# Loading two weight rows ahead of a branch, decoding late weights a step later, and moving sums, differences and splits a step sooner

## The chip, the core and the metric

One core of a Trainium2 chip runs the whole program in one launch. The metric is the device time of that launch in microseconds; a lower time is better. Times before are 1471.26 to 1475.34 us over three runs, median 1472.84.

## What is computed

Three layers follow one another on 4608 tokens of width 512:

```python
kv = einsum("bhsd,bhse->bhde", k, v); o = q @ kv; x = o / rms(o) * g_norm     # 8 batches, 8 heads, 576, 64
e = argmax(x @ w_gate + bias[modality]); x = p[e] * (relu(x @ w1[e]) @ w2[e])   # 8 experts, 512 -> 1024 -> 512
out = (sigmoid(x @ w_gate2) * (x @ w_val2)) @ w_out2                            # 512 -> 1536 -> 512
```

The change concerns the third layer, called the output part here, and the way into it. Its three weight matrices come as float64, that is as two 32-bit words an element.

## The kernel before

All matrix products are float32. Each is made of three products of halves: a value is split into a high part (a copy by ScalarE, ACT) and a low part (value minus high part, by VectorE, DVE), and TensorE (PE) multiplies high by high, high by low and low by high.

**Decoding.** The float64 weights are decoded in units of 128 x 512 (class `Decode`): one ACT instruction for the exponent, five on DVE for the words, and a store of 256 KB to `w_d[cb]` in DRAM. Most units are decoded during the expert layer. The last eight, those of `w_d[2]`, are `Late` units: `decode_late` loads the raw words (512 KB, L1646) and `decode_late2` decodes a unit and stores it (L155, L157), during the first steps of the output part.

**The output part** goes over 5 token blocks of 12 steps each, steps 0 to 59 (`NJ` is 12, `FIRST` is 24, `NU` is 60). Step 0 is computed around a branch (`tc.If`, L1206) that holds expert work that is rarely needed and not run here. Each step has eight spots in the order `SPOTS`; at each spot `prepare(s, spot)` issues what later steps need, then PE's product of that spot follows. A step of the first block (`glu_plain`, L984 to L986) is 24 matmuls for gate and value and 12 for the output, all 128 x 512. From the second block on (`glu_unit`, L1010 to L1012) a step computes its two products by seven smaller ones, in the order 1, 6, 7, 5, 2, 4, 3, of 6 matmuls each; DVE adds the banks of PE into `u2`, `u3` and `gm` (L1014).

**Weights.** `load_rows(s + 2)` (L1290) loads 512 KB of decoded weights for step s + 2 from `w_d` into one of two buffers, `rows[s % 2]`, at spot 0 of step s. `group` splits them for the next step into `wt` on ACT (L972) and DVE (L973) and stores the result for later blocks to `wt_d` (L1316). From step 12 the splits are of sums of the rows (`sum_w`, L1306). `load_raw` (L922) loads 256 KB of `w_out`; its split is stored to `wo_d` (L1347). All these transfers, and the loads of the next block's tokens (`load_y`, L1613), are issued by SyncE on one queue (SPq), in the order of the program. Each of them also waits for the transfer that used its lane (`DMAHW0` to `DMAHW7`) before.

**Y sums.** A block from the third on needs seven combinations of its tokens (`y_step`, L1253 for the low part of a split, L1257 for a sum). The table `YPLAN` says at which step and spot each is issued: keys are (step within the block before, spot), letters name the combination. `YPLAN[1]` serves the third block, made in steps 22 to 24. Buffers for the splits come from `free_y`, filled by `hold_y`.

**The tail.** Blocks from the third on have their output in chunks of 12 matmuls 128 x 256 (`run_chunk`, L1488 to L1490), seven kinds n for six pairs m. `ready_chunk` splits a chunk's input (ACT `gh` L1457, DVE `gl` L1450) up to four spots ahead. `sum_g` (L1469, L1470) makes two sums of a pair; for the last block GpSimd (POOL) makes a difference for each pair (L1461 for m below 3, L1472 for the others). `combine` (L1513) adds finished banks into `u2` and `u7`. After step 59 come 24 chunks: n of 2 and 4 alternating for m 0 to 5, then n = 6, then n = 5. In the same stretch `last_split` (L1548) splits the six differences, and `last_products` (L1562 to L1567) ends the program.

What is issued around the late units, with the words of the kernel:

```python
if spot == 0:
    load_wt(s + 1)
    if s + 2 <= NJ:
        load_raw(s + 2, s + 1)
    load_rows(s + 2)
    decode_late(s)
```

Of the kernel before, what the change touches and what calls it, by code (L numbers as in the profile page):

```python
# [25 lines left out]
NB = 5  # L26
# [58 lines left out]
def attention_moe_glu_kernel(  # L85
# [962 lines left out]
    with ExitStack() as st:  # L1048
# [80 lines left out]
        for g in range(2):  # L1129
            later(8 + 2 * g, lambda g=g: split0(g))  # L1130
            later(13 + g, lambda g=g: split1(g))

        def gv_first(at):
# [77 lines left out]
    with ExitStack() as st:  # L1211
# [31 lines left out]
        free_y = []  # L1243
        yslots = []

# [13 lines left out]
        def y_step(b, what):  # L1259


            sub = ALU.subtract
            if what in SPLIT:
                split_y(b, SPLIT[what], {"a": y11, "b": y21, "c": y22, "g": y22, "h": y21, "i": y11, "k": y12}[what])
            elif what == "d":
                sum_y(y22, y22, y12, sub)
            elif what == "e":
                sum_y(y12, y12, y11, sub)
            elif what == "f":
                sum_y(y11, y22, y11, ALU.add)  # L1270
            elif what == "j":
                sum_y(y21, y21, y11, sub)
# [3 lines left out]
                  (11, 1): "h", (11, 3): "k"},  # L1276
                 {(10, 5): "c", (10, 2): "d", (10, 4): "e", (11, 1): "a", (11, 7): "f", (11, 5): "i", (11, 2): "g", (11, 4): "k",
                  (12, 1): "b", (12, 6): "jh"},
                 {(10, 5): "c", (10, 2): "d", (10, 4): "e", (11, 1): "a", (11, 7): "f", (11, 5): "i", (11, 2): "g",
# [142 lines left out]
        def place_chunks(b):  # L1422

            s0 = NJ * b
            early = [(6, 2, 4), (7, 2, 4), (8, 2, 4), (10, 2, 4), (11, 6, 5), (11, 2, 4)]
            if b == NPLAIN:
                early[0:3] = [(7, 2, 4), (8, 6, 5), (9, 2, 4)]
            for m, (j, *spots) in enumerate(early):
                for spot, n in zip(spots, (1, 7)):
                    chunk_at.setdefault((s0 + j, spot), []).append((b, n, m))  # L1430
                sum_at.setdefault((s0 + max(j + 1, 2 * m + 2), (1, 5)[m % 2]) if m < 3 else (s0 + NJ + 1, (1, 5, 4)[m - 3]), []).append((b, m))
            seq = [(b, n, m) for m in range(6) for n in (2, 4)] + [(b, n, m) for n in (6, 5, 3)[0:3 if b < NB - 1 else 2] for m in range(6)]
            for i, c in enumerate(seq):
                chunk_at.setdefault((s0 + NJ + i // 6, SPOTS[1 + i % 6]), []).append(c)
# [7 lines left out]
        def ready_chunk(q):  # L1442
# [16 lines left out]
            split_c[q] = (hi, lo)  # L1459
            if n == (2 if m < 3 else 0) and b == NB - 1:  # L1460
                nc.gpsimd.tensor_tensor(out=g[a12], in0=g[a12], in1=g[a11], op=ALU.subtract)  # L1461
# [5 lines left out]
        def sum_g(b, m):  # L1467
            g = G[b]
            nc.vector.tensor_tensor(out=g[2 * m, 1], in0=g[2 * m, 1], in1=g[2 * m + 1, 1], op=ALU.add)  # L1469
            nc.vector.tensor_tensor(out=g[2 * m, 0], in0=g[2 * m, 1], in1=g[2 * m, 0], op=ALU.subtract)  # L1470
            if b == NB - 1 and m > 2:
                nc.gpsimd.tensor_tensor(out=g[2 * m + 1, 0], in0=g[2 * m + 1, 0], in1=g[2 * m, 0], op=ALU.subtract)  # L1472

# [33 lines left out]
        def combine(b, n):  # L1507
# [24 lines left out]
            if n == 6:  # L1532
# [4 lines left out]
                later_o.extend([lambda: third(0), lambda: third(1)])  # L1537
                later_o.append(lambda: add(held["u7"], held["u7"], held["u2"]))
            if n == 5 and b == NB - 1:
# [123 lines left out]
        def decode_late(s):  # L1663

            for i in ((0, 1) if s == 0 else (s,) if 1 < s < 8 else ()):
                jobs[i] = Late(units[NEARLY + i], i)

        def decode_late2(s):
            if 1 <= s < 9:
                d = jobs.pop(s - 1)  # L1670
                d.exponent()
                d.words()
                d.finish()
                d.store()

        def prepare(s, spot):
# [3 lines left out]
            if spot == 0:  # L1680
                load_wt(s + 1)
                if s + 2 <= NJ:
                    load_raw(s + 2, s + 1)
                load_rows(s + 2)
                decode_late(s)
# [16 lines left out]
            if b + 1 < NB:  # L1702
                for what, do in TURNS[min(b, 1)].get((j, spot), ()):
                    what(b + 1, do)
                if s == 9 and spot == 0:
                    hold_y(mw[1].tile([128, 2, 2, 2, HC], F32R, tag="w2r1", name="w2r1"))
# [11 lines left out]
            sums_o(s, spot)  # L1718
            if (s, spot) == (FIRST, 0):
                yslots.extend(xp.tile([128, XW], F32, tag="xg", name="yr", bufs=4) for _ in range(2))  # L1720
                free_g.extend(xp.tile([128, XW], F32, tag="xg", name="yr", bufs=4)[:, 0:HC] for _ in range(2))
            if s == NU - 1 and spot in SPOTS[1:7]:
# [8 lines left out]
        load_raw(2, 1)  # L1731
        load_rows(2)
        for i in range(4):
            load_y(1, i)
        for i in range(4):
            number_y(1, i)
        decode_late(0)
        ready_o(1, 0)
# [17 lines left out]
        for s in range(NU, NU + 4):  # L1756
            for spot in SPOTS:
                chunk_step(s, spot)
                if s == NU + 2 and spot in SPOTS[1:7]:
                    last_split(SPOTS.index(spot) - 1)  # L1760
        last_products()
# [26 lines left out]
```

## Time and profile before

| what | value |
|---|---|
| median of three runs | 1472.84 us (1471.26 to 1475.34) |
| profiled execution | 1472.33 us |
| its span, first to last instruction | 1470.5 us |
| mean granted clock of PE | 0.992 |
| busy: PE, DVE, ACT, POOL | 96%, 69%, 46%, 18% |
| DMA | 365.34 MB, mean 248 GB/s |

The time of the profiled execution is 1.8 us above its span. The granted clock is a share of PE's full speed. Idle time in a row of the timeline stands in brackets with what ended it.

### The profile page before, as it was taken

The numbers are of one execution on the slowest core, as the hardware profiler recorded it, in microseconds if no ns is written. First come the engines' busy times: TensorE is split into PE (matmuls) and PEld (weight loads), VectorE is DVE, ScalarE is ACT, GpSimd is POOL, SyncE is SP. The second block draws the span as 40 slices with busy tenths as digits, with TensorE's granted clock in tenths as the row PEclk, the third lists the DMA queues.
The fourth block names the chain that finished last, engine by engine and source line by source line (L and its number), as shares of the span: only waits on it lengthen the run. The fifth ranks groups of instructions, "written<-read, shape, count | busy, mean of one in ns | idle before, by whom it ended". The sixth has DMA issues, their size and how long they took to land.

```text
span 1470.5 us, 24842 instructions
## 1 busy us (share of the span) xinstructions
PE 1417.6 (96%) x9302; PEld 1240.9 (84%) x9302; DVE 1009.5 (69%) x1592; ACT 677.6 (46%) x1080; POOL 269.7 (18%) x356
## 2 busy tenths in 40 slices
PE   6997999999999999989999999999999999999996
PEld 6886789999999998778888887888889888898896
DVE  1567868888888877647866676565876468655574
ACT  3676555556555556746433342332433235222241
POOL 1021122223121213111011101011024200131025
PEclk9999999999999999999999999999999999999999
DMA  9987599998985857689887656886666655565553
GB/s 297 332 302 248 184 318 309 267 327 284 302 287 187 289 164 241 235 273 335 317 337 255 243 194 248 327 285 232 208 215 221 207 203 186 196 215 199 193 162 111
DMA packets 189708, 365.34 MB, mean 248 GB/s; under 512 B 22544, under 2 KB 114448, under 8 KB 182416
## 3 DMA queue, kind: packets, MB, share of 16 engines
q1 hardware_dynamic: 177408, 330.37, 66.8%
q0 software_dynamic: 10816, 32.08, 6.0%
q8 instruction: 75, 1.23, 0.3%
q10 hardware_dynamic: 1360, 1.26, 0.3%
q14 instruction: 49, 0.40, 0.1%
HBM read 301.31 MB, written 74.93 MB: 256 GB/s over the span
## 4 chain that ended last, share of the span: by engine, by line
PE 52%; DMA 2%; DVE 1%; POOL 1%; issue 1%; ACT 0%; SPq 0%; another core or an unknown queue 0%; POOLq 0%; ACTq 0%; DVEq 0%
PE gv L1010 10%; PE gv L1011 10%; PE gv L1012 10%; PE ac L1490 4%; PE ac L1488 3%; PE ac L1489 3%; PE ac L1382 2%; PE ac L1383 2%; PE ac L1384 2%; PE gv L984 1%; PE gv L986 1%; PE gv L985 1%; PE tr L947 1%; DMA wos<-wp_d 1%; DMA rows<-w_d 1%
## 5 line engine op out<-in xcount | busy, mean ns | idle before, releaser
L279 PE MATMUL ph<-xh,w1h 128*128 128x256 f32 x576 | 167.2, 290 | 1.1 <-ACT w1h L235 1.1
L280 PE MATMUL ph<-xh,w1l 128*128 128x256 f32 x576 | 163.5, 284 | 0.9 <-DVE w1l L237 0.9
L281 PE MATMUL ph<-xl,w1h 128*128 128x256 f32 x576 | 163.5, 284 | 0.0
L1014 DVE TENSOR_TENSOR u<-u,gv 128x512 f32<-128x512 f32 x144 | 98.5, 684 | 78.5 <-PE gv L1012 77.8
L1488 PE MATMUL ac<-wos,gh 128*128 128x256 f32 x480 | 135.7, 283 | 2.3 <-ACT gh L1457 1.1
L1490 PE MATMUL ac<-wos,gl 128*128 128x256 f32 x480 | 136.3, 284 | 1.4 <-DVE gl L1450 1.3
L1489 PE MATMUL ac<-wos,gh 128*128 128x256 f32 x480 | 135.9, 283 | 0.0
L1010 PE MATMUL gv<-half,wt 128*128 128x512 f32 x336 | 132.2, 393 | 0.0
L1011 PE MATMUL gv<-half,wt 128*128 128x512 f32 x336 | 131.3, 391 | 0.0
L1012 PE MATMUL gv<-half,wt 128*128 128x512 f32 x336 | 131.0, 390 | 0.0
L279 PEld LDWEIGHTS ph<-xh,w1h 128*128 128x128 f32 x576 | 110.8, 192 | 3.0 <-ACT w1h L235 1.3
L280 PEld LDWEIGHTS ph<-xh,w1l 128*128 128x128 f32 x576 | 110.9, 193 | 2.8 <-DVE w1l L237 1.1
L281 PEld LDWEIGHTS ph<-xl,w1h 128*128 128x128 f32 x576 | 110.6, 192 | 0.0
L335 PE MATMUL py<-w2h,hh 128*128 128x512 f32 x272 | 106.9, 393 | 0.0
L336 PE MATMUL py<-w2l,hh 128*128 128x512 f32 x272 | 106.8, 393 | 0.0
L337 PE MATMUL py<-w2h,hl 128*128 128x512 f32 x272 | 106.0, 390 | 0.0
L1488 PEld LDWEIGHTS ac<-wos,gh 128*128 128x128 f32 x480 | 91.8, 191 | 7.2 <-issue 1.4
L1489 PEld LDWEIGHTS ac<-wos,gh 128*128 128x128 f32 x480 | 91.8, 191 | 3.7
L1490 PEld LDWEIGHTS ac<-wos,gl 128*128 128x128 f32 x480 | 91.8, 191 | 1.9 <-DVE gl L1450 1.8
L349 POOL DMA_INDIRECT y_d<-y,sidx x36 | 40.4, 1122 | 283.2 <-ACT y L345 110.5
L1043 ACT ACTIVATE u<-u 128x512 f32<-128x512 f32 x48 | 30.4, 633 | 134.1 <-DVE u L1014 134.1
L301 ACT ACTIVATE hh<-ph 128x512 fp32r<-128x512 f32 x68 | 40.6, 598 | 105.5 <-PE ph L281 105.5
(408 smaller groups left out, 3736.1 us busy)
## 6 DMA issues: line engine op xcount, KB each, us to landing
wt<-wt_d SPq DMA_DIRECT2D x36, 1536.0 KB
half<-in_moe_w_dram SPq DMA_DIRECT2D x96, 512.0 KB
w1r<-in_moe_w_dram SPq DMA_DIRECT2D x40, 512.0 KB
w2r<-in_moe_w_dram SPq DMA_DIRECT2D x40, 512.0 KB
wos<-wp_d SPq DMA_DIRECT2D x72, 256.0 KB
rows<-w_d SPq DMA_DIRECT2D x24, 512.0 KB
wt<-wt_d SPq DMA_DIRECT2D x48, 256.0 KB
wt_d<-wt SPq DMA_DIRECT2D x12, 1024.0 KB
```

The source lines that it names most:

```text
L279: nc.tensor.matmul(out=o, lhsT=bh[:, c, cs], rhs=hi[:, c, 0:n], start=(c == 0), stop=False)
L280: nc.tensor.matmul(out=o, lhsT=bl[:, c, cs], rhs=hi[:, c, 0:n], start=False, stop=False)
L281: nc.tensor.matmul(out=o, lhsT=bh[:, c, cs], rhs=lo[:, c, 0:n], start=False, stop=(c == KC - 1))
L335: nc.tensor.matmul(out=o, lhsT=hi[:, f, cs], rhs=bh[:, f, :], start=first, stop=False)
L336: nc.tensor.matmul(out=o, lhsT=hi[:, f, cs], rhs=bl[:, f, :], start=False, stop=False)
L337: nc.tensor.matmul(out=o, lhsT=lo[:, f, cs], rhs=bh[:, f, :], start=False, stop=last)
L1010: nc.tensor.matmul(out=o, lhsT=wh, rhs=yh[:, c, :], start=first and c == 0, stop=False, skip_group_check=True)
L1011: nc.tensor.matmul(out=o, lhsT=wh, rhs=yl[:, c, :], start=False, stop=False, skip_group_check=True)
L1012: nc.tensor.matmul(out=o, lhsT=wl, rhs=yh[:, c, :], start=False, stop=last and c == 1, skip_group_check=True)
L1488: nc.tensor.matmul(out=o, lhsT=gh[:, cs], rhs=wh, start=fresh and i % 2 == 0, stop=False, skip_group_check=True)
L1489: nc.tensor.matmul(out=o, lhsT=gh[:, cs], rhs=wl, start=False, stop=False, skip_group_check=True)
L1490: nc.tensor.matmul(out=o, lhsT=gl[:, cs], rhs=wh, start=False, stop=stop, skip_group_check=True)
```

## The change

1. The weight rows of steps 2 and 3 are loaded ahead of the branch (`later(12)` and `later(15)`); the loads of them behind the branch go.
2. The late units are loaded and decoded one step later: the first two raw loads move from ahead of step 1 into step 1, the decoding from steps 1 to 8 into steps 2 to 9, and the buffer that they use becomes free for Y splits at step 10, not 9.
3. For the third block, c, d, e and the sum f (F, now by halves into two buffers `extra_y`) are in step 22, a, I, g, k and b in step 23, and in step 24 only the difference J and its split H.
4. For the last block, the sums of pairs 3 to 5 are issued a step sooner, POOL's six differences all when the chunk n = 2 is made ready, the six last splits over two steps, and the sum of `u7` and `u2` in two halves.

```diff
@@ -1129,6 +1129,7 @@
         for g in range(2):
             later(8 + 2 * g, lambda g=g: split0(g))
             later(13 + g, lambda g=g: split1(g))
+            later(12 + 3 * g, lambda g=g: nc.sync.dma_start(out=rows[g], in_=w_rows(2 + g)))
...
+            elif what == "F":
+                for k in range(2):
+                    sum_y(extra_y[k], y22[:, k], y11[:, k], ALU.add)
+            elif what == "I":
+                hl = free_y.pop(0)
+                for k in range(2):
+                    nc.scalar.activation(out=hl[0][:, k], in_=extra_y[k], func=ACTF.Copy)
+                for k in range(2):
+                    sum_y(hl[1][:, k], extra_y[k], hl[0][:, k], sub)
+                Y[b, 6] = hl
+            elif what == "J":
+                for k in range(2):
+                    sum_y(y11[:, k], y21[:, k], extra_y[k], sub)
+            elif what == "H":
+                split_y(b, 4, y11)
...
-                 {(10, 5): "c", (10, 2): "d", (10, 4): "e", (11, 1): "a", (11, 7): "f", (11, 5): "i", (11, 2): "g", (11, 4): "k",
-                  (12, 1): "b", (12, 6): "jh"},
+                 {(10, 1): "c", (10, 6): "d", (10, 5): "e", (10, 4): "F", (11, 1): "a", (11, 6): "I", (11, 5): "g", (11, 2): "k",
+                  (11, 4): "b", (12, 1): "J", (12, 6): "H"},
...
-                sum_at.setdefault((s0 + max(j + 1, 2 * m + 2), (1, 5)[m % 2]) if m < 3 else (s0 + NJ + 1, (1, 5, 4)[m - 3]), []).append((b, m))
+                late = (s0 + NJ, (6, 5, 4)[m - 3]) if b == NB - 1 else (s0 + NJ + 1, (1, 5, 4)[m - 3])
+                sum_at.setdefault((s0 + max(j + 1, 2 * m + 2), (1, 5)[m % 2]) if m < 3 else late, []).append((b, m))
...
-            if n == (2 if m < 3 else 0) and b == NB - 1:
+            if n == 2 and b == NB - 1:
                 nc.gpsimd.tensor_tensor(out=g[a12], in0=g[a12], in1=g[a11], op=ALU.subtract)
...
-            if b == NB - 1 and m > 2:
-                nc.gpsimd.tensor_tensor(out=g[2 * m + 1, 0], in0=g[2 * m + 1, 0], in1=g[2 * m, 0], op=ALU.subtract)
...
-                later_o.append(lambda: add(held["u7"], held["u7"], held["u2"]))
+                if b < NB - 1:
+                    later_o.append(lambda: add(held["u7"], held["u7"], held["u2"]))
+                else:
+                    h7, h2 = ([held[z][:, 2 * k:2 * k + 2, :] for k in range(2)] for z in ("u7", "u2"))
+                    later_o.extend([lambda: add(h7[0], h7[0], h2[0]), lambda: add(h7[1], h7[1], h2[1])])
...
-            for i in ((0, 1) if s == 0 else (s,) if 1 < s < 8 else ()):
+            for i in ((0, 1) if s == 1 else (s - 1,) if 2 < s < 9 else ()):
                 jobs[i] = Late(units[NEARLY + i], i)
...
-            if 1 <= s < 9:
-                d = jobs.pop(s - 1)
+            if 2 <= s < 10:
+                d = jobs.pop(s - 2)
...
-                load_rows(s + 2)
+                if s > 1:
+                    load_rows(s + 2)
                 decode_late(s)
...
-                if s == 9 and spot == 0:
+                if s == 10 and spot == 0:
                     hold_y(mw[1].tile([128, 2, 2, 2, HC], F32R, tag="w2r1", name="w2r1"))
...
-            if (s, spot) == (FIRST, 0):
+            if (s, spot) == (NJ, 0):
                 yslots.extend(xp.tile([128, XW], F32, tag="xg", name="yr", bufs=4) for _ in range(2))
-                free_g.extend(xp.tile([128, XW], F32, tag="xg", name="yr", bufs=4)[:, 0:HC] for _ in range(2))
+                extra_y.extend(xp.tile([128, XW], F32, tag="xg", name="yr", bufs=4)[:, 0:HC] for _ in range(2))
+            if (s, spot) == (FIRST, 7):
+                free_g.extend(extra_y)
...
-        load_rows(2)
...
-        decode_late(0)
...
-                if s == NU + 2 and spot in SPOTS[1:7]:
-                    last_split(SPOTS.index(spot) - 1)
+                at = (NU + 1, 6), (NU + 1, 5), (NU + 1, 4), (NU + 2, 6), (NU + 2, 7), (NU + 2, 5)
+                if (s, spot) in at:
+                    last_split(at.index((s, spot)))
```

Three places show how this moves instructions. Line numbers of the changed kernel are higher by 1 to 19 for the same statement.

SyncE, before, from the end of step 6 to the start of step 8 of the output part: the store of a late unit (L157), the loads of raw `w_out` and of rows (L922, L1290), a raw late load (L1646) and the two stores of splits.

```order
L157 DMA w_d2_78<-w2r1_8548 128x512 [waits DMAHW5_49,DVE_49]
L922 DMA wo_8969<-w_d1_77 128x512 [waits DMAHW6_49]
L1290 DMA rows0_2674<-w_d2_78 128x1024 [waits DMAHW7_49]
L1646 DMA w2r1_8548<-in_moe2_w_out_dram 128x1024 [waits DMAHW0_49,Activation_49]
L1316 DMA wt_d7_86<-wt1_7729 128x1536 [waits DMAHW1_49,DVE_49]
L1347 DMA wo_d6_97<-wos_9021 128x1024 [waits DMAHW2_49,DVE_49]
L157 DMA w_d2_78<-w2r1_8548 128x512 [waits DMAHW3_49,DVE_49]
L922 DMA wo_9050<-w_d2_78 128x512 [waits DMAHW5_49,DMAHW4_49]
L1290 DMA rows1_2675<-w_d2_78 128x1024
```

The same stretch in the changed kernel, from the end of step 6 to the start of step 8.

```order
L157 DMA w_d2_78<-w2r1_8550 128x512 [waits DMAHW1_49,DVE_49]
L922 DMA wo_9042<-w_d2_78 128x512 [waits DMAHW2_49,DMAHW1_49]
L1306 DMA rows1_2675<-w_d2_78 128x1024
L1665 DMA w2r1_8550<-in_moe2_w_out_dram 128x1024 [waits DMAHW4_49,Activation_49]
L1332 DMA wt_d8_87<-wt0_8528 128x1536 [waits DMAHW5_49,DVE_49]
L1363 DMA wo_d7_98<-wos_9092 128x1024 [waits DMAHW6_49,DVE_49]
L157 DMA w_d2_78<-w2r1_8550 128x512 [waits DMAHW7_49,DVE_49]
L922 DMA wo_9109<-w_d2_78 128x512 [waits DMAHW7_49,DMAHW0_49]
L1306 DMA rows0_2674<-w_d2_78 128x1024
```

Before, the load `wo_9050` waits for lane 5, that of the store in the first row; now each `wo` load that reads `w_d2` waits for the lane of the store in the row ahead of it (lane 1, then lane 7).

DVE, before, in step 22 (`rows`/`wsum` are weights, `yraw` and `half0` the tokens' sums and a split, `u2`, `u3`, `gm` PE's results):

```order
L973 TENSOR_TENSOR wt1_7729<-wsum_10392,wt1_7729 128x2x256
L1014 TENSOR_TENSOR u2_10397<-u2_10397,gv_10410 128x512
L1351 TENSOR_TENSOR gl_10419<-gm5_8533,gh_10418 128x512
L1014 TENSOR_TENSOR u3_10398<-u2_10397,gv_10424 128x512
L1014 TENSOR_TENSOR gm7_8535<-u3_10398,gv_10432 128x512
L1253 TENSOR_TENSOR half0_7669<-yraw_8527,half0_7669 128x1024
L973 TENSOR_TENSOR wt1_7729<-wsum_10392,wt1_7729 128x2x256
L1257 TENSOR_TENSOR yraw_8527<-yraw_8527 128x2x512
L1014 TENSOR_TENSOR gm9_8537<-u2_10397,gv_10424 128x512
L1257 TENSOR_TENSOR yraw_8527<-yraw_8527 128x2x512
L1014 TENSOR_TENSOR u3_10479<-u2_10397,gv_10432 128x512
```

The same stretch in the changed kernel.

```order
L973 TENSOR_TENSOR wt1_7730<-wsum_10388,wt1_7730 128x2x256
L1254 TENSOR_TENSOR half0_7669<-yraw_8529,half0_7669 128x1024
L1014 TENSOR_TENSOR u2_10393<-u2_10393,gv_10408 128x512
L1367 TENSOR_TENSOR gl_10417<-gm5_8535,gh_10416 128x512
L1258 TENSOR_TENSOR yraw_8529<-yraw_8529 128x2x512
L1014 TENSOR_TENSOR u3_10394<-u2_10393,gv_10423 128x512
L1014 TENSOR_TENSOR gm7_8537<-u3_10394,gv_10431 128x512
L1258 TENSOR_TENSOR yraw_8529<-yraw_8529 128x2x512
L973 TENSOR_TENSOR wt1_7730<-wsum_10388,wt1_7730 128x2x256
L1014 TENSOR_TENSOR gm9_8539<-u2_10393,gv_10423 128x512
L1258 TENSOR_TENSOR yr_9380<-yraw_8529 128x512
L1258 TENSOR_TENSOR yr_9381<-yraw_8529 128x512
```

The split into `half0` and the first sum of `yraw` stood behind `u3_10398`; now they stand ahead of its counterpart `u3_10394`, and the two halves of F are new in this step.

DVE, before, in the tail, around the turn from the chunks n = 6 to n = 5 (`w1r1` is a last split, `wos` are `u2` and `u7`):

```order
L1450 TENSOR_TENSOR gl_15592<-wsum_11449,gh_15591 128x512
L1548 TENSOR_TENSOR w1r1_8580<-rows0_11447,w1r1_8580 128x512
L1513 TENSOR_TENSOR wos_11445<-wos_11445,ac0_15500 128x512
L1513 TENSOR_TENSOR wos_11445<-wos_11445,ac1_15501 128x512
L1450 TENSOR_TENSOR gl_15613<-gm10_8538,gh_15612 128x512
L1513 TENSOR_TENSOR ot_15616<-wos_11445,ac2_14735 128x512
L1548 TENSOR_TENSOR w1r1_8580<-gm11_8539,w1r1_8580 128x512
L1513 TENSOR_TENSOR ot_15626<-wos_11445,ac3_14736 128x512
L1513 TENSOR_TENSOR wos_11446<-wos_11446,wos_11445 128x1024
L1450 TENSOR_TENSOR gl_15651<-wsum_11449,gh_15650 128x512
```

The same stretch in the changed kernel.

```order
L1567 TENSOR_TENSOR w1r1_8579<-gm11_8541,w1r1_8579 128x512
L1467 TENSOR_TENSOR gl_15592<-wsum_11445,gh_15591 128x512
L1528 TENSOR_TENSOR wos_11441<-wos_11441,ac0_15502 128x512
L1528 TENSOR_TENSOR wos_11441<-wos_11441,ac1_15503 128x512
L1467 TENSOR_TENSOR gl_15611<-gm10_8540,gh_15610 128x512
L1528 TENSOR_TENSOR ot_15614<-wos_11441,ac2_14731 128x512
L1528 TENSOR_TENSOR ot_15622<-wos_11441,ac3_14732 128x512
L1528 TENSOR_TENSOR wos_11442<-wos_11442,wos_11441 128x512
L1467 TENSOR_TENSOR gl_15647<-wsum_11445,gh_15646 128x512
```

The last split now stands ahead of the adds on `ac0` and `ac1`, and one half of the add of `wos` stands ahead of `gl_15647`, where the whole stood ahead of `gl_15651`.

## Rows read from the trace of the kernel before

**Rows 1.** the page, part 1: busy us of each engine, share of the span
```profile
PE 1417.6 (96%) x9302; PEld 1240.9 (84%) x9302; DVE 1009.5 (69%) x1592; ACT 677.6 (46%) x1080; POOL 269.7 (18%) x356
```

**Rows 2.** timeline, SP's queue, POOL and PE, place A (start, us, engine line op, [idle before <-releaser])
```profile
633.25 1.75 SPq L1613 DMA_DIRECT2D yr<-y_d  x4
...
636.13 0.19 POOL L935 COPY oid<-yr 128x1 int32<-128x1 int32 x1 [7.69 <-DMA yr<-y_d]
...
649.49 1.97 PE L947 MATMUL tr<-ident,yr 128*128 128x128 f32 x8 [3.81 <-ACT yr L942]
```

**Rows 3.** windows: busy us by engine, granted clock, DMA share, GB/s
```profile
640.00:660.00 20.00, 16.19 (x70) 13.30 (x69) 9.91 (x17) 9.81 (x17) 2.21 (x4) 0.91 0.97 338
880.00:900.00 20.00, 16.88 (x63) 13.41 (x62) 12.09 (x17) 7.53 (x12) 4.65 (x7) 0.83 0.59 213
```

**Rows 4.** timeline, DVE and PE, steps 22 and 24
```profile
859.97 0.68 DVE L1014 TENSOR_TENSOR u<-u,gv 128x512 f32<-128x512 f32 x1
861.36 1.22 DVE L1253 TENSOR_TENSOR half<-yraw,half 128x1024 fp32r<-128x1024 f32 x1
...
861.15 0.39 PE L1010 MATMUL gv<-w2r,wt 128*128 128x512 f32 x1
...
886.94 1.22 DVE L1253 TENSOR_TENSOR w2r<-yraw,w2r 128x1024 fp32r<-128x1024 f32 x1 [1.12 <-ACT w2r L1252]
...
888.91 0.77 PE L1010 MATMUL gv<-w2r,wt 128*128 128x512 f32 x1 [3.12 <-DVE u L1014]
```

**Rows 5.** timeline, DVE, POOL and PE, the tail
```profile
1436.90 2.23 DVE L1548 TENSOR_TENSOR w2r<-yr,w2r 128x512 fp32r<-128x512 f32 x1
...
1437.29 1.28 POOL L1472 TENSOR_TENSOR gm<-gm,gm 128x512 f32<-128x512 f32 x1
...
1441.04 0.36 PE L1488 MATMUL ac<-wos,gh 128*128 128x256 f32 x1 [1.14 <-ACT gh L1457]
...
1443.86 1.22 DVE L1513 TENSOR_TENSOR wos<-wos 128x1024 f32<-128x1024 f32 x1
...
1445.73 0.39 PE L1490 MATMUL ac<-wos,gl 128*128 128x256 f32 x1 [1.34 <-DVE gl L1450]
```

**Rows 6.** timeline, SP's queue, stores of a decoded unit and row loads behind it
```profile
694.09 0.32 SPq L157 DMA_DIRECT2D w_d<-w2r  x1
...
694.94 0.44 SPq L1290 DMA_DIRECT2D rows<-w_d  x1
...
703.08 0.42 SPq L1290 DMA_DIRECT2D rows<-w_d  x1
```

**Rows 7.** timeline: PE's first matmuls of steps 6 to 9; ACT and DVE, first splits
```profile
678.09 0.48 PE L984 MATMUL gv<-half,wt 128*128 128x512 f32 x1
...
687.15 0.48 PE L984 MATMUL gv<-half,wt 128*128 128x512 f32 x1
...
695.40 0.39 PE L984 MATMUL gv<-half,wt 128*128 128x512 f32 x1
...
703.56 0.39 PE L984 MATMUL gv<-half,wt 128*128 128x512 f32 x1
...
692.48 1.15 ACT L972 ACTIVATE wt<-rows 128x512 fp32r<-128x512 f32 x2 [1.60 <-DMA rows<-w_d]
...
701.76 1.16 ACT L972 ACTIVATE wt<-rows 128x512 fp32r<-128x512 f32 x2 [2.78 <-DMA rows<-w_d]
...
708.67 1.15 ACT L972 ACTIVATE wt<-rows 128x512 fp32r<-128x512 f32 x2 [1.53 <-DMA rows<-w_d]
...
717.39 0.63 ACT L972 ACTIVATE wt<-rows 128x512 fp32r<-128x512 f32 x1 [2.09 <-DMA rows<-w_d]
...
702.43 0.69 DVE L973 TENSOR_TENSOR wt<-rows,wt 128x512 fp32r<-128x512 f32 x1 [0.22 <-ACT wt L972]
```

**Rows 8.** the page, part 6: DMA issues, KB each, us to landing
```profile
y_d<-y POOLq DMA_DIRECT2D x4, 264.0 KB, 3.5
...
y_d<-y,sidx POOLq DMA_INDIRECT x36, 5.7
```

More of the change, by code (lines that the diff above doesn't have):

```diff
@@ L1243, in attention_moe_glu_kernel @@
         free_y = []
-        yslots = []
+        yslots, extra_y = [], []
         def hold_y(t, lo=0):
```

## The prediction

> **What bounds the kernel now.** I read the page first: TensorE (PE) is busy 96% of a span of 1470.5 us [rows 1]. So the kernel can only become shorter where PE stands still, or works at the lower clock, in the 4%. I then read PE's waits in the timeline, and the granted clock by window. Three places lie inside what the change touches.
>
> *Place A*, step 3 of the output part, just after the branch. PE waits 3.81 us at 649.49 [rows 2], put down to the transpose's input, because ScalarE (ACT) is itself stuck behind the load of the weight rows for step 3. That load stands in SP's queue behind the four token loads of 633.25 [rows 2]. The window 640 to 660 shows a granted clock of 0.91 [rows 3]: 0.09 x 20 = 1.8 us more. A costs 3.81 + 1.8 = **5.6 us**.
>
> *Place B*, step 24, the first of the third block. PE waits 3.12 us at 888.91 for VectorE (DVE) to add u3, and the window 880 to 900 shows 0.83 [rows 3, 4]: 0.17 x 20 = 3.4. B costs **6.5 us**. DVE is late because a split of a Y sum (886.94, 1.22 us, after an idle 1.12 for ACT's half of that split) stands ahead of u3 [rows 4].
>
> *Place C*, the tail. PE waits at 1445.73 for a gl that stands on DVE behind a 1.22 us add at 1443.86 [rows 5], and a little before, at 1441.04, for a bank that DVE empties late [rows 5]: 1.50 and 1.30 us from matmul to matmul, with smaller waits **some 3.5 us** (an estimate).
>
> If all three went and nothing came in their place, the profiled execution of 1472.33 us (span 1470.5 and 1.8 around it) would be 1472.3 - 5.6 - 6.5 - 3.5 = 1456.7. The median of the runs shown, 1472.84, is 0.5 above the profiled one, so I add 0.5 at the end.
>
> **The change, part by part.**
>
> *Rows before the branch.* The rows for steps 2 and 3 are loaded ahead of the branch, where their buffers are free and other loads run; PE there does not wait for SP's queue, so I cost the two issues at nothing. After the branch, the row loads and the raw loads no longer stand ahead of or between the token loads and the weights. Nothing else is late at step 3 once the rows are there: A goes, **-5.6**.
>
> *Decode one step later.* Each of the eight late units is stored one step later, but the wo and row loads that read them stay where they were. The order of SP shows what follows: before, the wo load of a step waits for the store of the step before last (lane 5, with six rows between); now, from step 9's loads on, it waits for the store issued directly ahead of it (lane 1); the rows of step 8 already do. SP is in order, so the row load behind it waits too. In the trace the store is issued at 694.09 and the rows at 694.94, 0.85 us later [rows 6]. They reach ACT at 701.76 and the first group is ready at 702.43 + 0.69 = 703.12; PE starts step 9 at 703.56 [rows 7]. There is 0.4 us of slack, and the store's landing now comes into this chain.
>
> How long does a store of 256 KB take to land? The trace does not show this one. Nearest rows: four stores of 264 KB on POOL's queue take 3.5 us by the page, the scatters of y 5.7 [rows 8]; a load of 264 KB on SP's queue, the first of four, is issued at 633.25 and used at 636.13, at most 2.9 [rows 2]. I take 3.5, as the same direction and size, and keep 2.9 and 5.7 as ends. The Trainium skill, "DMA: Bandwidth & Descriptors", section "Anatomy of one DMA — SWDGE (gpsimd) path", gives a fixed 2.0 us plus bytes over 436 GB/s, an estimated 2.6; by it the stalls below would add to some 3.8 us in place of 6.4 and the time would be 1467.6. The 3.5 of the trace is longer, and nothing in it shows such a landing on SP's queue.
>
> With 3.5, the rows are issued 3.5 + 0.43 (one wo issue) - 0.85 = 3.1 us later against PE. What that costs I work out step by step, as the time from the start of step s-2 to the moment that step s's first group is ready (ACT's split + 1.36, as at step 9), against the two steps that PE takes [rows 7]:
> step 8: 692.48 + 1.36 - 678.09 = 15.75, + 3.1 = 18.8 against 17.3: stall 1.5.
> Step 9: 703.12 - 687.15 = 15.97, + 3.1 = 19.1 against 16.4 + 1.5: 1.1.
> Step 10: 708.67 + 1.36 - 695.40 = 14.6, + 3.1, + 1.15 because a raw load now runs beside it (from issue to ACT 703.08 to 708.67 without one, 694.94 to 701.76 with) [rows 6, 7]: 18.9 against 16.3 + 1.1: 1.4.
> Step 11: 717.39 + 1.36 - 703.56 = 15.2, + 3.1 = 18.3 against 16.3 + 1.4: 0.5.
> Step 12: its rows had no store ahead of them and now stand behind the last one; I put it at 1.8, between the stall of step 8 and the whole 3.1. Sum **+6.4**, and A nets +0.8 (with 2.9: -0.9; with 5.7, 5.3 us a turn: +7.5).
>
> *Y sums a step sooner.* DVE's order shows a split (c) and a sum (d) ahead of u3 in step 22. Each holds DVE 1.2 us; before, the first of them runs at 861.36, after u3, which starts at 859.97 and takes 0.68, and product 4 of step 22 starts at 861.15 [rows 4]. Now u3 starts near 859.97 + 2.4 and, as it waits a little for ACT's half of c, at 862.6: done at 863.3, **PE waits 2.2**. In step 23, where a split and the two halves of I stand ahead of u3, the same walk gives 0.7; in step 24 J's halves are done before and only H stands ahead of u3: 0.2. B: -6.5 + 3.1 = **-3.4**. That holds if an idle of 2.2 us leaves the clock; the ones of 3.12 and 3.81 did not, the ones of 1.30 and 1.50 did. If the clock falls there, B is about -0.4; if DVE is ahead of my walk, up to -6. The two buffers for F are taken from the four of the token loads at step 12 instead of 24; one load a step then has two buffers, each free after a step's flip, and costs nothing unless a flip falls a step behind. The buffer of the late units, free for Y splits a step later, is first taken in step 10's splits, which run off PE's path.
>
> *Tail.* The add at 1443.86 is split in two and the six last splits come earlier: the gl at 1445.73 is free 1.2 us sooner, the bank at 1441.04 perhaps 0.9. Against that, all six sums and three of POOL's subtractions come into the first twelve chunks. A pair of chunks is some 2.9 us on PE (24 matmuls, 0.12 us apart); DVE needs two gl and two sums, 4 x 0.60, and loses some 1.3 to POOL: its split at 1436.90 took 2.23 us in place of 0.69 while POOL subtracted at 1437.29 [rows 5]. That is 3.7 a pair, 0.8 too much in each of three pairs, less DVE's lead. I take **0** (-2.5 to +2). POOL only moves work that it did anyway.
>
> **Sum.** +0.8 - 3.4 + 0 = -2.6: 1469.7 for the profiled execution, **1470.2** on the scale of the median. A measurement of this kernel can tell about 0.3%, 4.4 us: faster is below 1468.4, slower above 1477.3.
>
> **Rivals.**
> 1. *The store lands within 2.9 us, as the load does, and DVE's lead covers a part of u3's delay.* For it: the load's 2.9 has POOL's start in it. Against it: the 3.5 of POOL's stores. Stalls 4.7 and A -0.9, B -4.5, C 0: 1472.8 - 5.4 = **1467.4**. Chance 0.24. The 2.6 estimated from the Trainium skill's page "DMA: Bandwidth & Descriptors" falls under this case.
> 2. *All three waits vanish*: the late store is covered and DVE's order is harmless: 1456.7 + 0.5 = **1457**. Against it: 0.4 us of slack at step 9. Chance 0.10.
> 3. *Slower: the late store becomes the bound of steps 8 to 12.* With a landing of 5.7 (as the scatters), the stalls are 3.7, 1.2, 3.6, 0.6 and 4.0 = 13.1, A nets +7.5, and idles over 3 us lower the clock as at A and B (1.8 to 3.4 us more). With B -3.4: 1472.8 + 7.5 - 3.4 + 2.5 = **1479.5**. It decides from a landing of about 5 us. Chance 0.14.
> 4. *The new wait in step 22 lowers the clock*: +3, **1473**. Chance 0.07.
> That the change doesn't do what it says is excluded: the rows in both orders have moved as told.
>
> **How the numbers follow.** The forecast has 0.45. Faster: rivals 1 and 2 and a little of the forecast, 0.36. Slower: rival 3 and a little of the tail's upper end, 0.16. Same: 0.48. The forecast's own range is 1466.5 to 1475; the range for 8 in 10 takes in rival 1 and most of rival 3, 1464 to 1478.5, and leaves out rival 2 and the worst of rival 3.
>
> **What would show it.** Right: no idle over 1 us in step 3 and clock 1.0 there; idle of 0.5 to 2 us on PE at the starts of steps 8 to 12, with rows issued 3 us or more after a store; at step 22 an idle near 2.2 us put down to u3; none over 0.5 in step 24; the tail's two waits smaller, but new ones of 0.6 in the first twelve chunks. Wrong: rows issued within 1.5 us of the stores in steps 7 to 10, or an idle of 3 us and a low clock in step 22.

## The result, and the profile after

The changed kernel is slower: a median of 1482.58 us over four runs (1481.01 to 1484.73) against 1472.83 for the kernel before, ratio 1.0062 with a 95% interval of 1.0048 to 1.0076. The forecast of 1470.2 and its range, which ended at 1478.5, were too low; 2.6 us were to be gained, and 9.8 were lost.

The profiled execution took 1484.73 us, and its span is 1482.9, which is 12.4 us over the span before. To see where these lie, I matched the matmuls of the two traces one by one, since PE does the same ones in the same order, and noted in us by how much each starts later:

| stretch (time in the kernel before) | late at its start | late at its end | difference |
|---|---|---|---|
| attention, before anything that was changed | 0 | 3.9 | +3.9 |
| A, step 3 (649 to 653) | 3.9 | 0.9 | -3.0 |
| steps 8 to 12 (695 to 731) | 0.9 | 14.9 | **+14.0** |
| B, steps 22 and 23 (861 to 874) | 14.9 | 19.6 | +4.7 |
| B, step 24 (888 to 895) | 19.6 | 13.4 | -6.2 |
| up to the tail | 13.4 | 12.5 | -0.9 |
| tail | 12.5 | 12.3 | -0.2 |

The first row belongs to the execution and not to the change: the part ahead of the output part differs by up to 4 us from one profile to the next, though no edit touches it. The rest is in the windows of the changed kernel (busy us by engine, granted clock, DMA share, GB/s), to be held against [rows 3]:

```profile
640.00:660.00 20.00, 17.94 (x84) 14.49 (x83) 9.21 (x15) 9.89 (x17) 5.51 (x8) 1.00 0.84 310
700.00:720.00 20.00, 14.26 (x60) 11.00 (x59) 11.19 (x19) 5.15 (x9) 0.00 (x0) 0.96 0.81 276
720.00:740.00 20.00, 18.26 (x71) 13.27 (x69) 15.89 (x25) 8.22 (x13) 0.00 (x0) 0.95 0.72 247
740.00:760.00 20.00, 18.83 (x76) 15.40 (x77) 15.86 (x27) 8.33 (x14) 4.59 (x7) 0.91 0.93 342
860.00:880.00 20.00, 17.98 (x79) 14.48 (x78) 14.77 (x23) 7.57 (x13) 0.00 (x0) 0.97 0.41 149
880.00:900.00 20.00, 19.54 (x82) 15.71 (x81) 14.75 (x21) 7.74 (x12) 0.00 (x0) 0.94 0.54 190
```

Before, PE was busy for the whole of 700 to 760, with the clock at 1.00, and the 16 DMA engines were busy for nine tenths of 680 to 720:

```profile
680.00:700.00 20.00, 20.00 (x94) 16.66 (x93) 16.21 (x26) 12.65 (x21) 0.00 (x0) 1.00 0.91 325
700.00:720.00 20.00, 20.00 (x90) 16.57 (x89) 16.23 (x24) 8.98 (x15) 0.00 (x0) 1.00 0.90 327
```

Now three windows there are short of work and of clock. PE's timeline names the waits, first in step 3, then at the starts of steps 10 and 12, then in steps 22 and 23. The second row is ACT's, whose split of the rows of step 10 holds PE up:

```profile
651.59 1.27 PE L947 MATMUL tr<-ident,yr 128*128 128x128 f32 x8 [2.06 <-ACT yr L942]
...
718.13 1.15 ACT L972 ACTIVATE wt<-rows 128x512 fp32r<-128x512 f32 x2 [9.80 <-DMA rows<-w_d]
...
718.82 0.79 PE L984 MATMUL gv<-half,wt 128*128 128x512 f32 x1 [5.74 <-ACT wt L972]
...
741.17 0.50 PE L1010 MATMUL gv<-half,wt 128*128 128x512 f32 x1 [2.58 <-DMA wt<-wt_d]
...
878.22 0.50 PE L1010 MATMUL gv<-w2r,wt 128*128 128x512 f32 x1 [2.02 <-DVE u L1014]
...
892.84 0.50 PE L1010 MATMUL gv<-w2r,wt 128*128 128x512 f32 x1 [0.46 <-DVE u L1014]
```

The 5.74 us come from SP's queue where it issues the loads for steps 9 to 11; this answers to [rows 6]. L157 is the store of a late unit, and the next `wo` load (L922) is not issued until that store has landed:

```profile
694.94 0.32 SPq L157 DMA_DIRECT2D w_d<-w2r  x1
699.10 0.32 SPq L922 DMA_DIRECT2D wo<-w_d  x1
699.47 0.42 SPq L1306 DMA_DIRECT2D rows<-w_d  x1
...
703.08 0.32 SPq L157 DMA_DIRECT2D w_d<-w2r  x1
709.78 0.32 SPq L922 DMA_DIRECT2D wo<-w_d  x1
710.15 1.14 SPq L1306 DMA_DIRECT2D rows<-w_d  x1
711.38 0.39 SPq L1665 DMA_DIRECT2D w2r<-in_moe_w_out_dram  x1
711.87 0.38 SPq L1332 DMA_DIRECT2D wt_d<-wt  x1
712.34 0.38 SPq L1363 DMA_DIRECT2D wo_d<-wos  x1
712.81 2.13 SPq L157 DMA_DIRECT2D w_d<-w2r  x1
723.11 0.32 SPq L922 DMA_DIRECT2D wo<-w_d  x1
```

The waits are 4.2, 6.7 and 10.3 us (and 4.8 for the last store), where the sum of the prediction had 3.5 for each. The reader should see the bunch ahead of 712.81: once SP is held up until 709.78, it issues five transfers of 256, 512, 512, 768 and 512 KB within 3 us, and the next store comes behind all of them. At the 276 GB/s of this window these 2.6 MB alone are 9.5 us, as an estimate. From the release to the landing, the DMA engines moved what amounts to these five and the store (13.33 us at 218 GB/s, 2.9 MB). Just before the release and just before the landing they stood almost still:

```profile
709.00:710.00 1.00, 1.00 (x6) 0.81 (x6) 0.97 (x2) 0.00 (x0) 0.00 (x0) 1.00 0.13 41
709.78:723.11 13.33, 7.59 (x28) 5.82 (x27) 5.99 (x10) 2.87 (x5) 0.00 (x0) 0.87 0.64 218
722.00:723.00 1.00, 1.00 (x6) 0.82 (x5) 1.00 (x3) 0.45 (x1) 0.00 (x0) 1.00 0.08 31
```

So DMA engines that were nearly full before now stand idle while SP waits, and then get all of the step's traffic at once. Why they move it at 218 GB/s on the mean, where 650 to 654 shows 406, is not shown.

### The profile page after: what moved, and what is told of

Same layout as the page of the kernel before. It is cut to its first block, busy times and chain, and to the rows that moved or that the text cites. A ratio compares the mean times of both kernels' runs of the same rounds, so it can differ in the third digit from the quotient of the medians.

```text
span 1482.9 us, 24852 instructions
## 1 busy us (share of the span) xinstructions
PE 1426.1 (96%) x9302; PEld 1244.9 (84%) x9302; DVE 1011.9 (68%) x1596; ACT 678.0 (46%) x1081; POOL 270.3 (18%) x356
## 4 chain that ended last, share of the span: by engine, by line
PE 51%; DVE 2%; DMA 2%; POOL 1%; issue 0%; ACT 0%; SPq 0%; POOLq 0%; DVEq 0%; ACTq 0%
PE gv L1010 10%; PE gv L1011 10%; PE gv L1012 10%; PE ac L1505 4%; PE ac L1504 4%; PE ac L1503 4%; PE ac L1398 2%; PE ac L1400 2%; PE ac L1399 2%; PE tr L947 1%; PE gv L984 1%; PE gv L986 1%; PE gv L985 1%; DMA w_d<-w2r 1%; DMA rows<-w_d 1%; DMA wt<-wt_d 0%
```

## The experiments

Ratios are to the kernel before, run on the same chip beside each kernel, with their 95% intervals. The changed kernel has 1.0062. Differences between two runs are of their medians; runs on different chips are better compared by their ratios. "Theory Q" is: the loads wait for the late store, and the store waits for what the DMA engines were given ahead of it.

### The late decode alone, taken away and put in

In the first run the late decode goes back to the steps of before, and all else stays changed:

```diff
-            for i in ((0, 1) if s == 1 else (s - 1,) if 2 < s < 9 else ()):
+            for i in ((0, 1) if s == 0 else (s,) if 1 < s < 8 else ()):
...
-            if 2 <= s < 10:
-                d = jobs.pop(s - 2)
+            if 1 <= s < 9:
+                d = jobs.pop(s - 1)
...
+        decode_late(0)
...
```

> The changed kernel with the late decode at the steps of before (raw loads 0 and 1 ahead of step 1, stores in steps 1 to 8); the rest as changed. Theory Q (the row and wo loads of steps 8 to 12 wait on SP's queue for a store issued directly ahead of them, and that store lands only after the traffic queued ahead of it): no idle of PE over 1 us in steps 8 to 12, some 14 us less, 1467 to 1470. Rival T (the loss in steps 9 to 12 is from the traffic that the row loads before the branch shifted, not from the store): the idle stays and the time is above 1478.

Measured: 1470.25 us, ratio 0.9980 (0.9968 to 0.9993), 12.3 us under the changed kernel and at the upper end of theory Q's range, and PE has no wait over 0.2 us from step 4 to step 21. The second run is the opposite: the kernel before with this edit alone.

> The kernel before with the late decode one step later and nothing else. Theory Q: the loss of steps 9 to 12 comes with this edit alone, 12 to 14 us, less 1 to 2 that step 3 gains because the two raw loads are no longer ahead of its rows: 1483 to 1486. Rival (the loss needs the row loads ahead of the branch as well, which let steps 2 to 7 run earlier against the decode): under 1478.

Measured: 1481.70 us, ratio 1.0050 (1.0031 to 1.0070), a little under the range of theory Q and above the rival's. Its waits stand at the same two places, for 5.6 and 2.7 us, and SP's waits for the stores are 4.3, 6.8, 10.1 and 4.9 us. From step 8 to step 12 PE falls back by 12.5 us, against 14.0. So this edit, with nothing else, makes the loss of these steps; the row loads ahead of the branch are not needed for it. It also gives step 3 as much as the changed kernel has there, which is taken up below:

```profile
651.39 1.27 PE L947 MATMUL tr<-ident,yr 128*128 128x128 f32 x8 [2.06 <-ACT yr L942]
```

### What the store waits for

Three runs keep the late decode as changed and differ in what stands ahead of the store. First, the raw load of a late unit (512 KB) is issued behind the store of the step:

```diff
             if spot == 0:
...
-                decode_late(s)
+                if s == 1:
+                    decode_late(s)
...
             if spot == 3:
                 decode_late2(s)
+                if s > 1:
+                    decode_late(s)
```

> The changed kernel with the raw load of a late unit issued behind the store of the step (end of the step) and not ahead of it. Theory Q: the store has 512 KB less queued ahead of it, at the 276 GB/s of that stretch 1.9 us less, for each of four or five stores: steps 8 to 12 lose 5 to 10 us less, 1473 to 1478. Rival F (a store on this queue lands after a fixed time whatever lies ahead): 1481 to 1484.

Measured: 1478.22 us, ratio 1.0027 (1.0011 to 1.0042), 4.4 us under the changed kernel, at the slow end of theory Q's range and clear of rival F's. Steps 8 to 12 lose 8.8 us in its trace and not 14.0. Second, the stores of the late units go to POOL's queue, where nothing stands ahead of them, by a `store` of their own in `Late`:

```diff
+            def store(self):
...
+                    nc.gpsimd.dma_start(out=w_d[cb][:, :, lo:lo + 128], in_=self.f.rearrange("p (j f) -> p j f", f=128))
+                else:
+                    nc.gpsimd.dma_start(out=w_d[cb][:, c, 1024:1536], in_=self.f)
```

> The changed kernel with the stores of the late units on POOL's queue and not on SP's. Theory Q in its narrow form (the store is late because it stands in one queue behind some 1.8 MB of raw loads and stores): it lands in 3 to 4 us, the loss of steps 8 to 12 falls from 14 to about 6 us, 1474 to 1477. Rival B (all queues share the 16 engines' bandwidth, and the store gets its turn no sooner from another queue): landing 4 to 10 us as before, 1481 to 1485.

Measured: 1479.91 us, ratio 1.0052 (1.0034 to 1.0069): a small gain at most. The time lies between the ranges of the two; the landings, 4.2 to 8.1 us, are those of rival B. Third, the unit is decoded and stored two spots earlier in the step:

```diff
-            if spot == 3:
+            if spot == 2:
                 decode_late2(s)
```

> The changed kernel with the late unit decoded and stored two spots of the step earlier (spot 2, not 3), some 2.5 us; the step stays the changed one. Theory Q: what counts is the time from the store to the loads behind it; with 2.5 us of it covered, and fewer stores of splits queued ahead, the loss of steps 8 to 12 falls from 14 to 4 to 8 us, 1472 to 1477. Rival (DVE's five instructions at that spot hold up the splits that PE waits for, which takes their place): 1480 to 1485.

Measured: 1490.93 us, ratio 1.0109 (1.0087 to 1.0132), slower than all others. The rival held in its direction, but its range ended at 1485. In its list of PE's waits (in total, times, longest) the first line is new:

```profile
PE ac L1399 <- DVE wos L1362: 10.3, 6, 2.0
```

The five instructions of the decode now stand on DVE ahead of the split of `wos` that the step's output product needs. That holds PE up six times, by 2.0 us at most, and with the low clock after these idles PE falls back by 21 us from step 4 to step 12. But this run shows best what a store costs by itself, as here the split's stores to `wt_d` have gone earlier and the one to `wo_d` comes behind:

```profile
708.72 0.32 SPq L1332 DMA_DIRECT2D wt_d<-wt  x1
711.69 0.32 SPq L157 DMA_DIRECT2D w_d<-w2r  x1
712.30 0.32 SPq L1363 DMA_DIRECT2D wo_d<-wos  x1
713.75 0.32 SPq L922 DMA_DIRECT2D wo<-w_d  x1
```

From the issue of the store to the issue of the `wo` load that waits for it, for the four loads of steps 7 to 10:

| kernel | us from store to load |
|---|---|
| as changed | 4.16, 6.70, 10.30, 4.79 |
| as changed, old table of Y sums (the same order on SP) | 4.25, 7.37, 8.56, 6.02 |
| raw load behind the store | 2.86, 4.70, 5.04, 3.62 |
| store on POOL's queue | 4.19, 6.54, 8.14, 4.20 |
| store two spots earlier | 2.03, 2.06, 2.04, 2.03 |

The same 256 KB take 2.0 us when little is under way and up to 10.3 behind 2.6 MB. The second row shows how far two executions of the same order differ. A queue of its own changes little: its 8.1 us are near the 8.6 of the second row, and there the 512 KB for `wo_d` were issued behind the store, at 708.71 after 708.22. So the narrow form of theory Q, the place in SP's queue, falls. What fits all five rows is the backlog of the 16 engines, whichever queue it came by; less of it ahead shortens the wait.

### The other three edits

The two row loads ahead of the branch, in the kernel before and with nothing else:

> The kernel before with only the two row loads moved ahead of the branch. Theory: PE's wait in step 3 falls from 3.8 to about 2.1 us (the chain gm, gh, yr, transpose that remains) and the clock stays up there, 3 to 4 us less: 1469 to 1470. Rival (the raw loads of 512 KB, which stay in front of step 3's transfers, were what made it late): no change, 1472 to 1473.

Measured: 1471.34 us, ratio 0.9989 (0.9977 to 1.0000), between the two ranges: some 1.6 us by the ratio, where 3 to 4 were expected. The trace says why. The wait in step 3 is 2.54 us, the clock falls after it, and PE gains 1.0 us:

```profile
648.86 1.56 PE L947 MATMUL tr<-ident,yr 128*128 128x128 f32 x8 [2.54 <-ACT yr L942]
...
650.00:652.00 2.00, 2.00 (x7) 1.61 (x7) 0.35 (x1) 1.30 (x3) 0.00 (x0) 0.50 0.90 215
```

The old table of Y sums in the changed kernel (one line of `YPLAN` put back):

> The changed kernel with the old table of Y sums for the third block. Theory: the changed table trades 6.0 us in step 24 for 4.6 in steps 22 and 23, so this one is 1 to 2 us slower than the changed kernel, about 1484. Rival (the new order on DVE costs as much as it saves or more): 1480 to 1482.5.

Measured: 1481.33 us, ratio 1.0056 (1.0038 to 1.0074). The time is in the rival's range, and its interval overlaps that of the changed kernel. The gain of 1.5 us that the table at the top shows for B leans on one profile of the old order, that of the kernel before. In the three others with the old table (this run, the row loads alone, the late decode alone) step 24 has the same wait of 3.1 us, but the clock is back sooner, and B is 1.2 us shorter. Against those the new table gains 0.3 us. The times can't tell it from none.

The table with c, d, e and F behind u3 in step 22 and I behind u3 in step 23, on the run with the decode put back:

```diff
-                 {(10, 1): "c", (10, 6): "d", (10, 5): "e", (10, 4): "F", (11, 1): "a", (11, 6): "I", (11, 5): "g", (11, 2): "k",
+                 {(10, 5): "c", (10, 2): "d", (10, 4): "e", (10, 3): "F", (11, 1): "a", (11, 7): "I", (11, 5): "g", (11, 2): "k",
```

> The changed kernel with the late decode of before, and with c, d, e and F of the third block behind u3 in step 22 and I behind u3 in step 23. Theory (each combination that stands ahead of u3 on DVE is paid by PE, in step 22 with the lower clock too): the waits of 2.2 and 0.6 us go and step 24 stays without one, 4.6 us less than the run with the late decode of before alone, about 1465.7. Rival (the seven combinations do not fit between the two u3 of steps 22 and 24, and J or H comes late): PE waits in step 24 again, 1469 to 1471.

Measured: 1464.87 us, ratio 0.9951 (0.9935 to 0.9967), 5.4 under the run with the decode put back alone (4.3 by the ratios), as expected. Its windows at the place of B are full, with the clock up:

```profile
860.00:880.00 20.00, 20.00 (x90) 16.57 (x89) 18.69 (x26) 8.99 (x14) 0.00 (x0) 1.00 0.54 192
880.00:900.00 20.00, 20.00 (x90) 16.55 (x89) 14.80 (x24) 6.65 (x11) 4.78 (x7) 1.00 0.87 319
```

The tail's sums and POOL's differences put back, also with the decode put back:

> The changed kernel with the late decode of before, and with the tail's sums and POOL's differences where they were before; the last splits and the two half adds stay as changed. Theory (the earlier sums and differences cost 0.7 us in each of three pairs of chunks, the splits and the half adds gain 2.2): no waits on gl in the first twelve chunks, 2 us less than the run with the late decode of before alone, about 1468.2. Rival (the gain came from the earlier sums): the two waits at the turn to n = 5 come back, 1470 to 1472.

Measured: 1470.55 us, ratio 0.9985 (0.9970 to 1.0000), no gain. The trace lost the small waits of the first twelve chunks, but has larger ones at the two turns, and from 1283 (on the scale of the kernel before) to the end it is 1.5 us longer than the tail as changed:

```profile
1427.47 0.38 PE L1507 MATMUL ac<-wos,gl 128*128 128x256 f32 x1 [0.88 <-DVE gl L1467]
...
1438.45 0.36 PE L1505 MATMUL ac<-wos,gh 128*128 128x256 f32 x1 [2.08 <-ACT gh L1474]
```

By the trace the rival held: the earlier sums are worth their price. The times can't tell the two apart.

### The version that beats both

Step 3 kept a wait of 2.06 us. ACT weighs the first two token tiles (L942) behind the split of the step's result, which needs PE's last matmul. Weighing at spot 2, ahead of that split, was tried with the last two edits together, and then with the table alone and the tail as changed:

```diff
-            for at, what in plan + [((p + 2 + p // 2, 2 if p else 4), weigh_y), ((p + 2 + p // 2, 4 if p else 3), flip_y)]:
+            for at, what in plan + [((p + 2 + p // 2, 2), weigh_y), ((p + 2 + p // 2, 4 if p else 3), flip_y)]:
```

> Both edits of the two runs before on the late decode of before, and the weighing of the first two token tiles two spots earlier, ahead of the split of the step's result on ACT. Theory: the 2.1 us that are left in step 3 are the chain gm, gh, yr, transpose, and go with it: 1470.3 - 4.6 - 2.1 - 2.1 = about 1461.5. Rival (the gate gathers of POOL land later than ACT comes there): step 3 keeps a wait of 1 to 3 us, 1463 to 1465.

> The same with the differences on POOL, as changed. Theory (the two tiles weighed earlier save the 2.1 us left in step 3): 1464.9 - 2.1 = 1462.8. Rival (the wait for the gates takes their place): 1464.9, no gain over the run with u3 first.

Measured: 1463.42 us, ratio 0.9945 (0.9924 to 0.9966), and 1463.37 us, ratio 0.9932 (0.9918 to 0.9945). In both, PE's transposes in step 3 follow without a wait. So the rival's wait did not come; what the first lacks on its forecast is the gain that putting the tail's sums back was to bring. In the second:

```profile
648.95 1.04 PE L947 MATMUL tr<-ident,yr 128*128 128x128 f32 x8
```

Last, the six differences of the tail on DVE and not on POOL:

```diff
-                nc.gpsimd.tensor_tensor(out=g[a12], in0=g[a12], in1=g[a11], op=ALU.subtract)
+                nc.vector.tensor_tensor(out=g[a12], in0=g[a12], in1=g[a11], op=ALU.subtract)
```

> The late decode of before, c to F and I behind u3, the first two tiles weighed earlier, the tail as changed, but the six differences of the last block on DVE in place of POOL. Theory (in the first twelve chunks DVE is the bound: each pair costs it 2 gl, 2 sums and 1.1 us in which its sum is held up while POOL subtracts, 3.6 us against 2.9 of PE; a subtraction of its own costs 0.6): the waits of 0.6 to 0.75 us for gl fall to about 0.2 each, 1.5 us less than with POOL, about 1461. Rival (DVE has no room for six more instructions): the waits stay or grow, and it is equal to the run with POOL or slower, 1462.5 to 1464.

Measured: 1463.26 us, ratio 0.9935 (0.9922 to 0.9949). The trace has the three small waits at 0.12 to 0.13 us in place of 0.5, and the tail 0.7 us shorter than with POOL; the times cannot tell the two apart, and are in the rival's range. All three keep the row loads ahead of the branch and have the late decode where it was before. They are 0.6 to 0.7% under the kernel before and 1.2 to 1.3% under the changed one.

## Why the prediction was wrong, step by step

**Rows before the branch** (-5.6): -3.0. "Nothing else is late at step 3 once the rows are there" was wrong. Behind the row wait stood a chain that I had not followed: PE's last product, `gm` on DVE, `gh` on ACT, the weighing of `yr` on ACT, the transposes. It sets a floor of 2.06 us, which the earlier weighing took away. Nor do the -3.0 belong to this edit: the row loads alone leave 2.54 us and gain 1.0, the late decode alone, which takes two raw loads of 512 KB from ahead of step 3's rows, leaves 2.06 and gains 3.0. In the kernel before, these two raw loads (L1646) stand between the token loads of [rows 2] and the rows of step 3 (L1290):

```profile
635.04 0.90 SPq L1646 DMA_DIRECT2D w2r<-in_moe_w_val_dram  x2
...
637.08 0.56 SPq L1290 DMA_DIRECT2D rows<-w_d  x1
```

**Decode one step later** (+6.4): +14.0. This is the step that failed. The mechanism was the right one (the store directly ahead, SP in order, the rows late), and so was the direction of the third rival; the size of the term was wrong, in two ways.

The first is the landing. I asked how long a store of 256 KB takes and took one number from stores of that size elsewhere, 3.5 us. There is no such number: 2.0 alone, 3.2 to 10.3 here. And the waits feed each other: a held-up queue issues its transfers in a bunch, and the next store lands behind that bunch. The place was off too. I had a stall in each step from 8 to 12. But while SP waits, the engines run empty, and the rows of step 9 reached ACT 4.2 us after their issue in place of 6.8 [rows 6, 7], so that steps 8 and 9 lost nothing. Steps 10 and 12 lost 5.74 and 2.58. At step 12 it was not the sums of rows that came late but the load of `wt`, in SP's queue behind the last store. In all PE stood idle for 8.5 us, where the stalls of the sum come to 6.4.

The second is larger: the other 5.5 of the 14.0 us are PE at the lower clock after these two idles, which the sum put at nothing here, though it had priced the clock at A and B and in the third rival. In the changed kernel, after the one and the other:

```profile
720.00:722.00 2.00, 2.00 (x7) 1.57 (x6) 2.00 (x4) 0.74 (x2) 0.00 (x0) 0.54 0.30 118
...
743.00:745.00 2.00, 2.00 (x6) 1.59 (x5) 2.00 (x3) 0.83 (x2) 0.00 (x0) 0.50 0.97 397
```

**Y sums** (-3.4): -1.5. The waits were as worked out, 2.0 and 0.5 idle for 2.2 and 0.7, and none in step 24 for 0.2. The clock was the part left to a condition, and it fell, as the fourth rival said. That was a matter of the execution: of the six profiles with this wait it fell in four. The 6.5 us that B was said to cost came from one profile too; in three others the old table costs 5.0. A late u3 makes the wait before and after; with it ahead, B is 6.2 us shorter than in the profile before, and 4.7 shorter than with the table as changed.

**Tail** (0): -0.2. The new waits of 0.6 in the first chunks came, as three idles of 0.5 us, and so did the gains at 1441.04 and 1445.73, 1.0 us each for 0.9 and 1.2. POOL's subtraction and DVE's sum stand against each other as in [rows 5]; L1486 takes 1.78 us, where it takes 0.68 in the run with the differences on DVE, and the gl behind it is late for PE:

```profile
1432.10 1.67 POOL L1478 TENSOR_TENSOR gm<-gm,gm 128x512 f32<-128x512 f32 x1 [1.96 <-DVE gl L1467]
```

```profile
1432.54 1.78 DVE L1486 TENSOR_TENSOR gm<-gm,rows 128x512 f32<-128x512 f32 x1
1434.35 0.69 DVE L1487 TENSOR_TENSOR gm<-gm,gm 128x512 f32<-128x512 f32 x1
1434.96 0.68 DVE L1467 TENSOR_TENSOR gl<-yr,gh 128x512 fp32r<-128x512 f32 x1
```

```profile
1435.70 0.39 PE L1505 MATMUL ac<-wos,gl 128*128 128x256 f32 x1 [0.50 <-DVE gl L1467]
```

**The chances.** The third rival, with 0.14, is what happened, in its direction and its cause; its stalls of 13.1 us and its 2.5 for the clock were in fact 8.5 and 5.5, so that its 1479.5 came near partly by luck, and the lower clock in step 22, the fourth rival, came on top. Its condition, a landing over 5 us, was measured against the scatters of y; it should have been worked out from the queue: the order of SP shows what is issued ahead of each store, and the windows give the GB/s at which it drains. The 2.6 us estimated from the Trainium skill, "DMA: Bandwidth & Descriptors", section "Anatomy of one DMA — SWDGE (gpsimd) path", is a fit for transfers that GpSimd issues; it is near the 2.03 of SP's store with little under way, and no guide to one that stands behind a backlog.

## What to carry to other kernels

When a change brings a load next to the store that it reads, price the wait by the bytes issued ahead of the store over the measured GB/s, not by the store's own size, and let the next turn start from the bunch that the wait leaves. Look first at how full the DMA engines are: at 0.9, as here, there is little room to make up for the time in which the queue stands still. Give each idle of PE that comes out of the sum a price for the clock as well; here it made 5.5 of 14.0 us. On an in-order queue such a step of distance is slack worth keeping, even if each transfer seems hidden. And after taking away the wait that ended last, follow the chain of the next one: it is often a fixed chain through three engines, and moving one instruction ahead of it may be worth as much.

## What the runs showed of the hardware that was not expected

A store of the same size, from the same buffer, landed in 2.03 to 2.06 us with little under way, and in 10.3 behind 2.6 MB; on POOL's queue still in up to 8.1.

Idles of PE of the same length were treated differently. After 2.06 us in step 3 of the changed kernel the granted clock stayed at 1.00 (646 to 658); after 2.02 us in step 22 it fell, and PE's matmuls there stood 0.43 us apart in place of 0.23, which is the lower of the clock's two levels:

```profile
650.00:654.00 4.00, 2.41 (x14) 2.00 (x15) 2.07 (x4) 3.56 (x6) 0.00 (x0) 1.00 1.01 406
...
876.00:880.00 4.00, 1.98 (x6) 1.41 (x6) 3.90 (x5) 1.12 (x2) 0.00 (x0) 0.86 0.00 0
880.00:884.00 4.00, 4.00 (x14) 3.20 (x13) 2.56 (x5) 0.00 (x0) 0.00 (x0) 0.72 0.68 229
```

It is not the place that tells them apart. With the old table of Y sums, the same idle of 2.06 us in step 3 did lower the clock (first row); with the decode and the tail's sums put back, the same idle of 2.01 us in step 22 did not (second row, with that idle in it):

```profile
652.00:654.00 2.00, 2.00 (x6) 1.54 (x6) 1.90 (x4) 0.00 (x0) 0.00 (x0) 0.50 0.43 170
...
861.00:869.00 8.00, 5.99 (x27) 4.68 (x26) 6.52 (x9) 1.12 (x2) 0.00 (x0) 1.00 0.33 111
```

Over the profiles of all runs, the idle of 2.05 to 2.07 us in step 3 lowered the clock in four of nine, for 1.6 us, and that of 2.0 us in step 22 in four of six, for another 1.6 us. So what an idle of this length costs in one profile says little about the next execution. No run shows what decides it.
